# Routing tokens to expert slots in passes of four 128-token tiles that run across batch borders

## The chip, the cores and the metric

The kernel runs on one core of one Trainium2 chip. A core has five engines that work side by side and wait for each other through semaphores: TensorE (PE in the profile; its weight loads are PEld), VectorE (DVE), ScalarE (ACT), GpSimd (POOL) and SyncE (SP, which here only issues DMAs). TensorE writes into PSUM, a small memory of eight banks; the other operands live in SBUF. The metric is the device time of one execution in microseconds (us), lower is better; times of several runs are given by their median.

## The reference

Attention over 8 batches, 8 heads, 576 positions and 64 dimensions, with a window of 128 positions, feeds a soft mixture of experts over all 8 x 576 = 4608 tokens of width 512:

```python
scores = scale * q @ k.T;  scores = where(in_window, scores + bias, -1e9)
attn = exp(scores - max); attn /= sum;  x = (attn @ v) -> [4608, 512]
logits = x @ phi                                   # 32 slots: 8 experts x 4
d = softmax(logits, over tokens);  slot_input = d.T @ x          # [32, 512]
slot_out[e] = relu(slot_input[e] @ w1[e]) @ w2[e]                # 4 rows each
c = softmax(logits, over slots);   return c @ slot_out           # [4608, 512]
```

The softmax over tokens runs over all batches at once, so `slot_input` is built up along the way with a running maximum, a running sum and a rescaled accumulator.

## The kernel before, in words

**Attention.** The work is cut into 72 groups `(b, t, g)`: batch `b`, tile `t` of 128 positions (the fifth, `t = 4`, has the last 64), and half of the heads `g` (the fifth tile takes all heads in one group). That is 9 groups a batch. A loop runs one **round** per group. In round `i` PE does `flip` (L366, transposes of the probabilities of group i-3), `values` (L400, probabilities times v for group i-4) and `scores` (L253 and L260, or L241 and L246) for group i+1; DVE masks (L273 to L277), takes row maxima (L295) and normalises (L311); ACT copies the flipped probabilities out of PSUM (`split`, L373), takes exponentials (`expo`, L351) and copies finished attention outputs (`x_store`, L416); POOL masks the flipped copies (L375, L377) and prepares the sum (L303). SP issues the loads of q, k, v and, spread over the rounds, 36 expert weights of 512 KB.

**Slots.** When a tile of x is complete, `x_flip` (L428) transposes it on PE, and `x_keep` (L437, ACT) copies it out. `flip` and `x_flip` write halves of one PSUM tile, `pq`. When all tiles of a batch are there, a **pass** for this batch begins and takes one step a round: `logits` (L446, four tiles side by side in four strips of 32 rows, the "lanes"), `token_copy` (L464, ACT), `token_max` (L471, DVE), `slot_flip` (L480, PE), `token_exp` (L490 and L494, ACT), `token_sum` (L502, DVE), `token_flip` (L509, PE), `token_keep` (L518, ACT), `slots_max` (L552 and L553, DVE), `slot_sum` (L525, PE), `slots_exp` (L556, ACT), `slot_add` (L538, DVE) and `slots_norm` (L563 and L564 on DVE, L565 on POOL).

**The fifth tile.** The 64-token rests of two batches share one tile, `xt_t`, and belong to the pass of the odd batch (1, 3 and 5; the last batch has another order and its own code behind the loop). That pass has a fifth tile with steps of its own: `logits_tail` (L457), a second copy (L466), second transposes (L482, L511), and `slot_tail` (L532), a matmul that adds to the accumulator of `slot_sum`. Its `x_keep` stands behind `expo` on ACT.

**Order.** The order on each engine is the order in which the code is written: `do(when, i, fn, ...)` files a step under a place of round `i`, and `run(when, i)` writes it there: "pre" is ahead of the round's DVE work, "act" right behind `split`, "mid" and "pe" behind `scores` (ahead of and behind `expo`), "dve" at the end. `after_values` files the steps. After the loop come the last batch and the experts' matmuls.

Of the kernel before, what the change touches and what calls it, by code (L numbers as in the profile page):

```python
# [10 lines left out]
F32 = mybir.dt.float32  # L11
# [5 lines left out]
ALU = mybir.AluOpType  # L17
# [51 lines left out]
def tile_attn_softmoe(  # L69
# [369 lines left out]
    def lanes(b):  # L439
        return 4 if b < last else 2  # L440

    def logits(b):
        lp = ps_1.tile([P, 512], F32, tag="mi", name="lp")
        for j in range(NPAIR):
            for c in range(lanes(b)):
                nc.tensor.matmul(  # L446
                    lp[NS * c:NS * c + NS, 0:P], lhsT=phi[:, j], rhs=xts[c][:, j],
                    start=(j == 0), stop=(j == NPAIR - 1),
                )
        st["l", b] = lp  # L450

    def with_tail(b):
        return b % 2 and b < last

    def logits_tail(b):
        for j in range(NPAIR):
            nc.tensor.matmul(  # L457
                st["l", b][fin, P:2 * P], lhsT=phi[:, j], rhs=xt_t[:, j],
                start=(j == 0), stop=(j == NPAIR - 1),
            )  # L460

    def token_copy(b):
        lp, r = st.pop(("l", b)), NS * lanes(b)
        nc.scalar.copy(lg[0:r, 0:P], lp[0:r, 0:P])  # L464
        if with_tail(b):
            nc.scalar.copy(lg[fin, P:2 * P], lp[fin, P:2 * P])  # L466

    def token_max(b):
        r = NS * lanes(b)
        nm = work.tile([P, 1], F32, tag="nm", name="nm")  # L470
        nc.vector.tensor_reduce(  # L471
            nm[0:r], lgm[0:r, 3:4 + P * (2 if with_tail(b) else 1)], axis=AX.X, op=ALU.max, negate=True)
        st["n", b] = nm

    def slot_flip(b):
        r = NS * lanes(b)
        dp = ps_1.tile([P, 512], F32, tag="mi", name="dp")
        st["d", b] = dp
        lq = dp[:, 2 * P:]
        nc.tensor.transpose(lq[:, 0:r], lg[0:r, 0:P], ident[0:r, 0:r])  # L480
        if with_tail(b):
            nc.tensor.transpose(lq[:, P:P + NS], lg[fin, P:2 * P], ident[fin, fin])  # L482
        st["c", b], st["lm"] = lq, dp

    def token_exp(b):
        r = NS * lanes(b)
        m = P * (2 if with_tail(b) else 1)
        nm = st.pop(("n", b))
        sb = work.tile([P, 1], F32, tag="sb", name="sb")
        nc.scalar.activation(lg[0:r, 0:m], lg[0:r, 0:m], AF.Exp, bias=nm[0:r], scale=1.0, accum_out=sb[0:r])  # L490
        al = None
        if b:
# [13 lines left out]
    def token_flip(b):  # L506
        r = NS * lanes(b)
        dp = st["d", b]
        nc.tensor.transpose(dp[:, 0:r], lg[0:r, 0:P], ident[0:r, 0:r])  # L509
        if with_tail(b):  # L510
            nc.tensor.transpose(dp[:, P:P + NS], lg[fin, P:2 * P], ident[fin, fin])  # L511
# [3 lines left out]
    def token_keep(b):
        dn = work.tile([P, P + NS], F32, tag="dn", name="dn", bufs=1)
        m = P + NS if with_tail(b) else NS * lanes(b)
        (nc.scalar.copy if b < last else nc.vector.tensor_copy)(dn[:, 0:m], st["d", b][:, 0:m])  # L518
        st["d", b] = dn

    def slot_sum(b):
        dn = st["d", b]
        ap = ps_1.tile([P, DM], F32, tag="mi", name="ap") if b < last else pq[:, 0]
        for c in range(lanes(b)):
            nc.tensor.matmul(  # L525
                ap[NS * c:NS * c + NS], lhsT=dn[:, NS * c:NS * c + NS], rhs=xns[c],
                start=True, stop=(c < 3 or not with_tail(b)),
            )
        st["a", b] = ap

    def slot_tail(b):
        nc.tensor.matmul(st["a", b][fin], lhsT=st["d", b][:, P:], rhs=xn_of(b, 4), start=False, stop=True)  # L532

    def slot_add(b):
        ap, r = st.pop(("a", b)), NS * lanes(b)
        al = st.pop(("s", b))[0]
        if b:
# [4 lines left out]
    def rows(b):  # L542
        return slice(9 * (b // 2) + 4 * (b % 2), 9 * (b // 2) + 4 + 5 * (b % 2))

    def slots(b):
        return ln[:, rows(b)]

    def slots_max(b):
        m = 4 + b % 2
        src = st.pop(("c", b))[:, 0:NS * m].rearrange("p (i s) -> p i s", s=NS)  # L550
        cm = work.tile([P, 5], F32, tag="cm", name="cm")
        nc.vector.tensor_reduce(cm[:, 0:m], src, axis=AX.X, op=ALU.max)  # L552
        nc.vector.tensor_tensor(slots(b), src, bc(cm[:, 0:m], 2, NS), op=ALU.subtract)  # L553

    def slots_exp(b):
        nc.scalar.activation(slots(b), slots(b), AF.Exp)  # L556

    def slots_norm(b):
        m = 4 + b % 2
        cs = work.tile([P, 5], F32, tag="cs", name="cs")  # L560
        mul = (nc.gpsimd if b < last else nc.vector).tensor_tensor
        return [
            lambda: nc.vector.tensor_reduce(cs[:, 0:m], lne[:, rows(b)], axis=AX.X, op=ALU.add),  # L563
            lambda: nc.vector.reciprocal(cs[:, 0:m], cs[:, 0:m]),  # L564
            lambda: mul(slots(b), slots(b), bc(cs[:, 0:m], 2, NS), op=ALU.mult),  # L565
# [186 lines left out]
    def after_values(i, key):  # L752
# [9 lines left out]
        tail = with_tail(b)  # L762
        late = b > 0 and b % 2 == 0
        if p == 0 and late:
            do("mid", i + 3, x_flip, b, t)
            do("act", i + 4, x_keep, b, t)
        elif t < 4:
            do("pe", i + 1 + (p == 1 and late), x_flip, b, t)
            if b < last or p == 0:
                do("act", i + 2 + (p == 0 or p == 1 and late), x_keep, b, t)  # L770
        if p == (4 if b < last else 1):
            do("pe", i + 1, logits, b)
            if tail:
# [12 lines left out]
            do("act", i + 5, slots_exp, b)
            if tail:
# [6 lines left out]
            do("dve", i + 6, later, slots_norm, b)  # L794
# [351 lines left out]
```

## Time and profile before

| | |
|---|---|
| median of 3 runs | 301.19 us (300.13, 305.6, 301.19) |
| profiled execution | 298.23 us, span 296.5 us |
| mean granted TensorE clock | 0.979 |
| PE, DVE, ACT, POOL busy | 87%, 74%, 70%, 36% of the span |
| attention rounds | first exponential at 6.49 us, last at about 222 us |
| moved by DMA | 72.62 MB, 245 GB/s over the span |

The span runs from the first to the last instruction. The shares are means over stages with different limits: up to about 222 us four engines work on the rounds, and behind it PE works mostly alone on the experts. A line such as L446 is a line of the kernel before; the profile names a group of instructions by that line, its engine and its tiles.

### The profile page before, as it was taken

The numbers are of one execution on the slowest core, as the hardware profiler recorded it, in microseconds if no ns is written. First come the engines' busy times: TensorE is split into PE (matmuls) and PEld (weight loads), VectorE is DVE, ScalarE is ACT, GpSimd is POOL, SyncE is SP. The second block draws the span as 40 slices with busy tenths as digits, with TensorE's granted clock in tenths as the row PEclk, the third lists the DMA queues.
The fourth block names the chain that finished last, engine by engine and source line by source line (L and its number), as shares of the span: only waits on it lengthen the run. The fifth ranks groups of instructions, "written<-read, shape, count | busy, mean of one in ns | idle before, by whom it ended". The sixth has DMA issues, their size and how long they took to land.

```text
span 296.5 us, 13603 instructions
## 1 busy us (share of the span) xinstructions
PE 257.3 (87%) x5539; PEld 180.4 (61%) x5539; DVE 219.3 (74%) x502; ACT 207.4 (70%) x814; POOL 107.4 (36%) x222
## 2 busy tenths in 40 slices
PE   7587898988889998989889799786988989999980
PEld 3465675766567766757666577465756643587650
DVE  3899997998789999896988998596683444656450
ACT  3789997898789998888997889687684311044450
POOL 2055524543443655254544626365352012000000
PEclk9799999999999999999999999998999999999996
DMA  6736378859675995986797777766455579999996
GB/s 194 223 117 182 92 240 284 248 176 314 204 240 191 303 319 171 312 262 195 207 318 250 229 256 244 234 183 216 132 180 181 165 264 351 411 402 337 342 366 261
DMA packets 36755, 72.62 MB, mean 245 GB/s; under 512 B 4402, under 2 KB 15316, under 8 KB 36692
## 3 DMA queue, kind: packets, MB, share of 16 engines
q1 hardware_dynamic: 35972, 71.24, 72.4%
q8 instruction: 44, 0.72, 1.0%
q10 hardware_dynamic: 720, 0.51, 0.5%
q14 instruction: 19, 0.16, 0.2%
HBM read 62.29 MB, written 9.44 MB: 242 GB/s over the span
## 4 chain that ended last, share of the span: by engine, by line
PE 51%; DVE 19%; ACT 11%; POOL 9%; issue 6%; DMA 2%; DVEq 0%; ACTq 0%; POOLq 0%
PE xp L400 11%; ACT area L351 8%; PE s L260 6%; PE op L990 5%; PE hp L953 5%; DVE s L295 5%; DVE area L311 4%; PE po L1015 3%; PE pq L366 3%; POOL area L375 3%; PE s L253 3%; DVE s L273 3%; POOL area L377 2%; PE lp L446 2%; PE pq L428 2%
## 5 line engine op out<-in xcount | busy, mean ns | idle before, releaser
L351 ACT ACTIVATE area<-s,nb 128x128 f32<-128x128 f32 x286 | 102.4, 384 | 8.8 <-DVE nb L298 8.4
L400 PE MATMUL xp<-area 128*64 128x128 f32 (+1 forms) x1104 | 74.4, 273 | 11.2 <-POOL area L375 3.8
L400 PEld LDWEIGHTS xp<-area 128*64 128x64 f32 x1104 | 54.6, 138 | 20.3 <-POOL area L377 6.3
L351 ACT ACTIVATION_READ_ACCUMULATOR area<-s,nb 128x1 f32 x286 | 63.4, 222 | 0.0
L311 DVE TENSOR_TENSOR area<-area,rs 128x512 f32<-128x512 f32 (+1 forms) x73 | 61.2, 838 | 2.2
L373 ACT COPY area<-pq 128x512 f32<-128x512 f32 (+1 forms) x72 | 42.7, 594 | 18.9 <-PE pq L366 17.0
L295 DVE TENSOR_REDUCE s<-s 128x4 f32<-128x512 f32 x71 | 49.5, 698 | 2.2
L375 POOL TENSOR_SCALAR_AFFINE_SELECT area<-area 128x512 f32<-128x512 f32 x48 | 34.4, 717 | 31.2 <-ACT area L373 30.6
L260 PE MATMUL s<-kq 64*32 64x160 f32 x1792 | 44.0, 303 | 1.3 <-issue 1.1
L303 POOL TENSOR_SCALAR rs<-sm 128x4 f32<-128x4 f32 x70 | 14.0, 200 | 78.7 <-ACT area L351 77.4
L275 DVE COPY_PREDICATED s<-cst,s 128x512 f32<-128x512 int32 x48 | 33.1, 690 | 7.5 <-PE s L260 7.4
L366 PE MATMUL pq<-unit_r,area 64*128 64x64 f32 x552 | 31.1, 231 | 8.3 <-ACT area L437 4.8
L377 POOL TENSOR_SCALAR_AFFINE_SELECT area<-area 128x512 f32<-128x512 f32 x48 | 36.3, 756 | 3.3
L366 PEld LDWEIGHTS pq<-unit_r,area 64*128 64x128 f32 x552 | 23.0, 139 | 23.1 <-ACT area L437 8.3
L260 PEld LDWEIGHTS s<-kq 64*32 64x32 f32 x1792 | 30.1, 107 | 3.3 <-issue 2.7
L416 ACT COPY area<-xp 128x512 f32<-128x512 f32 (+1 forms) x37 | 20.8, 562 | 5.5 <-PE xp L400 5.1
L253 PE MATMUL s<-ramp,ones 64*32 64x320 bf16 x448 | 19.1, 311 | 3.9 <-ACT area L351 2.3
L437 ACT COPY area<-pq 128x512 f32<-128x512 f32 x34 | 20.8, 612 | 0.3 <-PE pq L422 0.3
L1017 ACT COPY ob<-po 128x512 f32<-128x512 f32 x19 | 10.4, 591 | 11.4 <-PE po L1015 11.4
L1017 DVE COPY ob<-po 128x512 f32<-128x512 f32 x17 | 11.2, 687 | 6.6 <-PE po L1015 5.7
L428 PE MATMUL pq<-unit_r,area 64*128 64x64 f32 x264 | 14.8, 232 | 1.1 <-ACT area L437 0.9
L307 DVE RECIPROCAL rs<-rs 128x4 f32<-128x4 f32 (+1 forms) x73 | 12.4, 169 | 4.2 <-POOL rs L303 3.5
(184 smaller groups left out, 329.9 us busy)
## 6 DMA issues: line engine op xcount, KB each, us to landing
w<-w SPq DMA_DIRECT2D x53, 512.0 KB, 5.3
out<-ob SPq DMA_DIRECT2D x36, 256.0 KB, 4.0
kq<-q_t SPq DMA_DIRECT2D x69, 128.0 KB, 3.5
kq<-k_t SPq DMA_DIRECT2D x32, 256.0 KB, 4.1
area<-v_n SPq DMA_DIRECT2D x31, 256.0 KB, 4.7
area<-w SPq DMA_DIRECT2D x8, 512.0 KB, 4.4
area<-v_n SPq DMA_DIRECT2D x12, 128.0 KB, 4.1
kq<-w SPq DMA_DIRECT2D x3, 512.0 KB, 5.4
```

The lines of the kernel that those rows point to most:

```text
L253: nc.tensor.matmul(s4[32 * c:32 * c + 32, 2 * par:2 * par + 2, 32 * r:32 * r + WIN], lhsT=ones[rows, 0:32], rhs=ramp[rows, h], start=True, ...
L260: nc.tensor.matmul(s4[32 * c:32 * c + 32, 2 * par + jj, 32 * r:32 * r + WIN], lhsT=qt[rows, 2 * h + jj if t == 4 else jj, 32 * r:32 * r + 32],
L275: nc.vector.copy_predicated(s4[:, :, P:2 * P], bc(mask_u, 1, 4), s4[:, :, 0:P])
L295: nc.vector.tensor_reduce(st[key]["mx"][:, us], merged(key, us), axis=AX.X, op=ALU.max, negate=True)
L311: nc.vector.tensor_tensor(p4, p4, bc(rs, 2, P), op=ALU.mult)
L351: nc.scalar.activation(s["p4"][:, u], merged(key, u), AF.Exp, bias=s["nb"][:, u:u + 1], scale=SCALE, accum_out=s["sm"][:, u:u + 1],)
L366: nc.tensor.transpose(s["pt"][:, u, r], s["p4"][rows, u], ident[rows, rows])
L373: nc.scalar.copy(pa[:, us].rearrange("p u (r w) -> p u r w", r=2), s["pt"][:, us])
L375: nc.gpsimd.affine_select(pp[:, us], pa[:, us], [[0, m], [-1, P]], ALU.is_gt, 0.0, base=0, channel_multiplier=1)
L377: nc.gpsimd.affine_select(pa[:, us], pa[:, us], [[0, m], [1, P]], ALU.is_ge, 0.0, base=0, channel_multiplier=-1)
L400: nc.tensor.matmul(xp[D * par:D * par + D, j, 0:w], lhsT=v_slot[b, t - 1 + ph][:, D * h:D * h + D], rhs=src[:, 2 * par + i] if t < 4 else ...
L1017: copy_by[by](ob, po)
```

## The change

The seven passes by batch (and the small one of the last batch) become eight passes by readiness (and the small one): the tiles of batches 0 to 6 are put in one list in the order in which they are complete, the shared 64-token tile being an entry like the others, and cut into fours across batch borders; the eighth has three. Every pass has lanes only, so the steps of the fifth tile go. The passes thus begin at other rounds: `logits` at rounds 12, 21, 28, 37, 44, 53, 60 and 66, where it was at 13, 22, 31, 40, 49, 58 and 67. Flips of x are filed at most one a round, at "pe", and each `x_keep` at "act" of the next round; flips for the next pass wait until `slot_sum` of the pass before has been written. `slot_add` is always at "dve" of its round (it was at "pre" for passes without a fifth tile).

```diff
+    tiles = [(b, t) for b in range(last) for t in range(4 + b % 2)] + [(last, 1), (last, 2)]
+    cuts = [4 * k for k in range(8)] + [len(tiles) - 2, len(tiles)]
+    passes = [tiles[a:z] for a, z in zip(cuts, cuts[1:])]
+    end = len(passes) - 1
+    pass_of = {key: (k, c) for k, p in enumerate(passes) for c, key in enumerate(p)}
...
-    def logits(b):
+    def logits(k):
         lp = ps_1.tile([P, 512], F32, tag="mi", name="lp")
         for j in range(NPAIR):
-            for c in range(lanes(b)):
+            for c, key in enumerate(passes[k]):
                 nc.tensor.matmul(
-                    lp[NS * c:NS * c + NS, 0:P], lhsT=phi[:, j], rhs=xts[c][:, j],
+                    lp[NS * c:NS * c + NS, 0:P], lhsT=phi[:, j], rhs=x_of(*key)[:, j],
...
-    def logits_tail(b):
-        for j in range(NPAIR):
-            nc.tensor.matmul(
-                st["l", b][fin, P:2 * P], lhsT=phi[:, j], rhs=xt_t[:, j],
...
-        if with_tail(b):
-            nc.scalar.copy(lg[fin, P:2 * P], lp[fin, P:2 * P])
...
-        if with_tail(b):
-            nc.tensor.transpose(dp[:, P:P + NS], lg[fin, P:2 * P], ident[fin, fin])
-            nc.gpsimd.memset(lg[0:64, P:2 * P], LOW)
-            nc.gpsimd.memset(lg[64:3 * NS, P:2 * P], LOW)
...
-    def slot_tail(b):
-        nc.tensor.matmul(st["a", b][fin], lhsT=st["d", b][:, P:], rhs=xn_of(b, 4), start=False, stop=True)
...
-        tail = with_tail(b)
-        late = b > 0 and b % 2 == 0
-        if p == 0 and late:
-            do("mid", i + 3, x_flip, b, t)
-            do("act", i + 4, x_keep, b, t)
-        elif t < 4:
-            do("pe", i + 1 + (p == 1 and late), x_flip, b, t)
...
-            if tail:
-                do("pe", i + 2, x_flip, b, 4)
-                do("pe", i + 4, x_keep, b, 4)
-                do("pe", i + 5, slot_tail, b)
-                do("dve", i + 5, slot_add, b)
-            else:
-                do("pre", i + 5, slot_add, b)
+        k, c = pass_of[b, t]
+        turn[0] = max(i + 1, turn[0] + 1, ready.get(k - 1, 0) + 4)
+        do("pe", turn[0], x_flip, b, t)
+        if (b, t) != tiles[-1]:
+            do("act", turn[0] + 1, x_keep, b, t)
+        if c == lanes(k) - 1:
+            ready[k] = i
+            do("pe", i + 1, logits, k)
...
+            do("dve", i + 5, slot_add, k)
```

Lines shift by the edit: in the changed kernel `flip` is L372, `values` L406, `scores` L266, `x_flip` L434, `logits` L452, `split` L379, `x_store` L422, `x_keep` L443, `token_copy` L460, `token_exp` L480 and L484, `token_keep` L503, `slots_exp` L536 and `expo` L357.

**PE, end of the round in which the pass over batch 1 begins.** Before, the round ended with `logits` and `logits_tail`, behind the scores of the next group and ahead of the next `flip` and `values`:

```order
L260 MATMUL s_1_84<-kq 32x160 x16
L446 MATMUL lp<-area,phi 32x128 x16
L457 MATMUL lp<-area,phi 32x128 x4
L366 MATMUL pq<-unit_r,area 128x64 x8
L400 MATMUL xp<-area 64x128 x4
```

Now the pass begins one round earlier, on the same round as the last flip of its x:

```order
L266 MATMUL s_0_83<-kq 32x160 x16
L434 MATMUL pq<-unit_r,area 128x64 x8
L452 MATMUL lp<-area,phi 32x128 x16
L372 MATMUL pq<-unit_r,area 128x64 x8
L406 MATMUL xp<-area 64x128 x4
```

The four matmuls of the fifth tile are gone from here; that tile is lane 0 of the next pass.

**ACT, from `token_exp` of the same pass to the second copy of x behind it.** Before:

```order
L490 ACTIVATE lg,sb<-lg,nm 128x256
L494 ACTIVATE al<-lg,nm 128x1
L351 ACTIVATE area,sm<-s_0_83,nb 128x128 x4
L373 COPY area<-pq 128x512
L518 COPY dn<-dp 128x160
L416 COPY area<-xp 128x512
L351 ACTIVATE area,sm<-s_1_84,nb 128x128 x4
L437 COPY area<-pq 128x512
L373 COPY area<-pq 128x512
L556 ACTIVATE ln<-ln 128x4x32
```

Now:

```order
L480 ACTIVATE lg,sb<-lg,nm 128x128
L484 ACTIVATE al<-lg,nm 128x1
L422 COPY area<-xp 128x4x64
L357 ACTIVATE area,sm<-s_0_83,nb 128x128 x4
L379 COPY area<-pq 128x512
L503 COPY dn<-dp 128x128
L357 ACTIVATE area,sm<-s_1_84,nb 128x128 x4
L379 COPY area<-pq 128x512
L536 ACTIVATE ln<-ln 128x4x32
L443 COPY area<-pq 128x512
L422 COPY area<-xp 128x512
```

The copy of the flipped fifth tile out of `pq` stood behind four exponentials (L437 behind L351); it now stands behind `split` and `slots_exp`, ahead of the exponentials.

**PE, near the end of the loop, where the last full pass begins.** Before, ahead of a `values` for batch 7 (the row L400) stood only a flip of x and the flip of the probabilities:

```order
L260 MATMUL s_1_84<-kq 32x160 x16
L428 MATMUL pq<-unit_r,area 128x64 x8
L366 MATMUL pq<-unit_r,area 128x64 x8
L400 MATMUL xp<-area 64x128 x8
L253 LDWEIGHTS ones
```

Now the logits of the last full pass, three lanes, stand ahead of it too; before, they came one round later, behind it:

```order
L266 MATMUL s_1_84<-kq 32x160 x16
L434 MATMUL pq<-unit_r,area 128x64 x8
L452 MATMUL lp<-area,phi 32x128 x12
L372 MATMUL pq<-unit_r,area 128x64 x8
L406 MATMUL xp<-area 64x128 x8
```

**ACT, where the passes take their copy of the logits.** Before, `token_copy` (L464) followed `split` directly, and a copy of x stood elsewhere; now, in the pass that begins at round 28:

```order
L379 COPY area<-pq 128x512
L443 COPY area<-pq 128x512
L460 COPY lg<-lp 128x128
L422 COPY area<-xp 128x512
L357 ACTIVATE area,sm<-s_0_83,nb 128x128 x4
```

One `x_keep` stands ahead of `token_copy` in the same round.

More of the change, by code (lines that the diff above doesn't have):

```diff
@@ L491, in token_exp @@
         al = None
-        if b:
+        if k:
             al = work.tile([P, 1], F32, tag="al", name="al")
@@ L504, in token_sum, with token_flip, token_keep, slot_sum @@
             nc.vector.tensor_copy(s_run, sb)
[L506 to L511, printed above, removed]
-            nc.gpsimd.memset(lg[0:64, P:2 * P], LOW)
-            nc.gpsimd.memset(lg[64:3 * NS, P:2 * P], LOW)
[L515 to L529, printed above, removed]
-    def slot_tail(b):
[L532 to L537, printed above, removed]
+    def token_flip(k):
+        r = NS * lanes(k)
+        nc.tensor.transpose(st["d", k][:, 0:r], lg[0:r, 0:P], ident[0:r, 0:r])
+    def token_keep(k):
+        dn = work.tile([P, P], F32, tag="dn", name="dn", bufs=1)
+        r = NS * lanes(k)
+        (nc.scalar.copy if k < end else nc.vector.tensor_copy)(dn[:, 0:r], st["d", k][:, 0:r])
+        st["d", k] = dn
+    def slot_sum(k):
+        dn = st["d", k]
+        ap = ps_1.tile([P, DM], F32, tag="mi", name="ap") if k < end else pq[:, 0]
+        for c in range(lanes(k)):
+            nc.tensor.matmul(
+                ap[NS * c:NS * c + NS], lhsT=dn[:, NS * c:NS * c + NS], rhs=xns[c], start=True, stop=True)
+        st["a", k] = ap
+    def slot_add(k):
+        ap, r = st.pop(("a", k)), NS * lanes(k)
+        al = st.pop(("s", k))[0]
+        if k:
             nc.vector.scalar_tensor_tensor(acc[0:r], acc[0:r], al[0:r], ap[0:r], op0=ALU.mult, op1=ALU.add)
@@ new lines, in after_values @@
+        if (b, t) not in pass_of:
+            return
+        k, c = pass_of[b, t]
[6 more added lines that the diff above has]
+            do("pe", i + 1, logits, k)
+            if k == end:
+                return
+            assert turn[0] <= i + 3
+            do("act", i + 2, token_copy, k)
+            do("dve", i + 2, token_max, k)
+            do("pe", i + 2, slot_flip, k)
+            do("act", i + 3, token_exp, k)
+            do("dve", i + 3, token_sum, k)
+            do("pe", i + 3, token_flip, k)
+            do("act", i + 4, token_keep, k)
+            do("pre", i + 4, slots_max, k)
+            do("pe", i + 4, slot_sum, k)
+            do("act", i + 5, slots_exp, k)
+            do("dve", i + 5, slot_add, k)
+            do("dve", i + 6, later, slots_norm, k)
@@ L796, in tile_attn_softmoe @@
+    turn, ready = [0], {}
     with tc.manual_schedule(engines=ORDERED):
@@ L837, in tile_attn_softmoe @@
         x_keep(last, 2)
-        token_copy(last)
+        token_copy(end)
         flip(gb, to=bank("pt"))
@@ L841, in tile_attn_softmoe @@
         split(gb, HI)
-        slot_flip(last)
-        token_max(last)
+        slot_flip(end)
+        token_max(end)
         values(ga)
@@ L851, in tile_attn_softmoe @@
         split(gc)
-        token_exp(last)
+        token_exp(end)
         total(gd, LO)
@@ L865, in tile_attn_softmoe @@
         split(gd, HI)
-        token_sum(last)
+        token_sum(end)
         x_store(last, 3)
@@ L869, in tile_attn_softmoe @@
         x_store(last, 4, nc.scalar)
-        token_flip(last)
+        token_flip(end)
         lane_rows(ps_1.tile([P, 512], F32, tag="xp", name="rows"))
@@ L880, in tile_attn_softmoe @@
         x_store(last, 0, js=slice(2, 4))
-        token_keep(last)
+        token_keep(end)
         x_flip(last, 3, free[0])
@@ L887, in tile_attn_softmoe @@
         lane_keep()
-        slot_sum(last)
+        slot_sum(end)
         load_weight()
@@ L897, in tile_attn_softmoe @@
         x_keep(last, 0)
-        slot_add(last)
+        slot_add(end)
         last_flip()
@@ L1040, in tile_attn_softmoe @@
         last_slot_flip()
-        slots_max(last)
-        slots_exp(last)
-        later(slots_norm, last)
+        slots_max(end)
+        slots_exp(end)
+        later(slots_norm, end)
         drain()
```

104 lines of the change are left out of this document (39 added, 65 removed).

## The prediction

> **What bounds the kernel now.** I read the page first: the busy shares, and the chain that ended last.
>
> ```profile
> PE 257.3 (87%) x5539; PEld 180.4 (61%) x5539; DVE 219.3 (74%) x502; ACT 207.4 (70%) x814; POOL 107.4 (36%) x222
> ...
> PE 51%; DVE 19%; ACT 11%; POOL 9%; issue 6%; DMA 2%; DVEq 0%; ACTq 0%; POOLq 0%
> ```
>
> PE carries half of the chain, DVE a fifth. These are averages over the span, so I cut the attention stage at the first exponential of every batch (nine rounds) and, inside a batch, took the five rounds in which `logits` to `slots_exp` stand. The columns are the stretch, its length, busy time of PE, PEld, DVE, ACT and POOL, granted clock, share of the DMA engines and GB/s.
>
> ```profile
> 85.17:110.13 24.96, 23.03 (x596) 17.14 (x592) 23.52 (x53) 23.36 (x97) 12.43 (x26) 1.00 0.81 261
> 110.13:138.48 28.35, 25.72 (x616) 18.74 (x612) 23.26 (x53) 23.64 (x99) 13.55 (x28) 1.00 0.78 249
> ...
> 66.74:85.17 18.43, 16.50 (x346) 11.80 (x338) 13.62 (x31) 14.27 (x58) 8.09 (x18) 1.00 0.79 259
> 120.66:138.48 17.82, 16.45 (x346) 11.90 (x338) 13.48 (x31) 14.16 (x59) 8.10 (x18) 1.00 0.85 271
> 175.75:193.85 18.10, 16.56 (x398) 11.52 (x392) 13.42 (x31) 14.13 (x58) 8.09 (x18) 1.00 0.79 258
> 95.64:110.13 14.49, 13.94 (x326) 10.24 (x318) 13.80 (x31) 13.48 (x57) 7.68 (x16) 1.00 0.94 307
> ```
>
> The last row is a pass without a fifth tile, the three above it are the passes with one. In the last row PE, DVE and ACT are busy for 96%, 95% and 93% of the time: that is what five rounds cost when nothing stands in the way. With the fifth tile they take 18.12 us in the mean, 3.63 us more, and DVE is idle for 4 to 5 us of them though its work is the same. So the passes with a fifth tile are held up by something that is short on DVE and ACT. Outside the rounds nothing of the change is left: behind 241 us the chain is the experts' matmuls, and I take that part as it is.
>
> **The change part by part.** *The fifth tile goes.* The chain over the pass of batch 1 (start, length, what) shows its four PE steps, and the timeline of PE shows a wait of `flip` in each of the three passes.
>
> ```profile
> 66.86 1.08 PE lp L446 x32
> 67.94 0.87 PE lp L457 x8
> ...
> 70.60 0.26 PE dp L480
> 70.86 0.18 PE dp L482
> ...
> 74.56 0.26 PE dp L509
> 74.82 0.19 PE dp L511
> ...
> 81.78 0.99 PE ap L532 x2
> ```
>
> ```profile
> 79.38 0.46 PE L366 MATMUL pq<-unit_r,area 64*128 64x64 f32 x8 [1.18 <-ACT area L437]
> ...
> 132.69 0.46 PE L366 MATMUL pq<-unit_r,area 64*128 64x64 f32 x8 [1.37 <-ACT area L437]
> ...
> 187.78 0.46 PE L366 MATMUL pq<-unit_r,area 64*128 64x64 f32 x8 [1.54 <-ACT area L437]
> ```
>
> One lane alone costs PE nearly what four cost (0.87 against 1.08 us in the logits, 0.99 in `slot_tail`), and the transposes 0.18 and 0.19: 2.23 us a pass. The wait comes from `x_keep` of the fifth tile: it stands behind four exponentials on ACT, and the next `flip` writes the same PSUM tile. At "act" it runs right behind `split` and `slots_exp`, and PE meets it with its scores done as in every other round: 1.36 us in the mean. Together 3.59 us, which agrees with the 3.63 from the windows. Three passes: **-10.8 us**. The floor under that is the last window above: DVE and ACT are then the next to be late, with about 1 us of slack each in five rounds. Bounds: -10.8 if all of it is free, and by the DMA (below) -7.5.
>
> *One more pass comes.* The trace does not show a pass added, but shows what one puts on the chain; this is the pass over batch 4, from its first to its last step.
>
> ```profile
> 149.71 1.01 PE lp L446 x32
> ...
> 156.07 0.26 PE dp L509
> ...
> 159.25 1.04 PE ap L525 x8
> 160.32 0.75 DVE acc L538
> ...
> 166.71 0.19 DVE cs L563
> ...
> 167.67 0.40 POOL ln L565
> ```
>
> That is 3.65 us. Below, it could cost nothing, if PE's parts fall into DVE's turns and the other way round; no gain is possible. Above, the steps of DVE that are not on this chain come on top:
>
> ```profile
> L502 DVE SCALAR_TENSOR_TENSOR fine<-fine,al,sb 128x1 f32<-128x1 f32 x6 | 3.5, 583 | 0.0
> ...
> L553 DVE TENSOR_TENSOR ln<-dp,cm 128x128 f32<-128x128 f32 x4 | 1.2, 292 | 0.1
> L552 DVE TENSOR_REDUCE cm<-dp 128x4 f32<-128x128 f32 x4 | 1.1, 285 | 0.3 <-PE dp L509 0.3
> ```
>
> 0.58, 0.29 and 0.29 make 4.8 us. With engines at 93 to 96% little is hidden, so I take the row of the whole pass: **+3.6 us**.
>
> *The last full pass starts ahead of a DMA wait.* Near the end of the loop `values` of batch 7 waits for v, whose loads are issued at the slot's release, and PE then runs slowly:
>
> ```profile
> 205.68 1.55 PE L400 MATMUL xp<-area 128*64 128x128 f32 x12 [2.35 <-DMA area<-v_n]
> ...
> 208.62 1.17 PE L446 MATMUL lp<-area,phi 128*32 128x128 f32 x32
> ...
> 206.00:207.00 1.00, 1.00 (x12) 0.83 (x8) 0.00 (x0) 0.15 (x2) 0.19 (x1) 0.50 0.16 44
> 207.00:208.00 1.00, 1.00 (x35) 0.65 (x40) 0.00 (x0) 0.00 (x0) 0.00 (x0) 0.50 0.00 0
> 208.00:209.00 1.00, 1.00 (x36) 0.49 (x24) 0.17 (x1) 0.00 (x0) 0.00 (x0) 0.57 0.00 0
> ```
>
> The logits (about 1.1 us) stood behind that wait, on the chain; now they stand ahead of it and fill 1.1 of its 2.35 us: -1.1. The wait itself stays, since the loads are where they were. The granted clock is 0.50, 0.50 and 0.57 in the 3 us behind the wait, so 3 - 1.57 = 1.43 us are lost there. Idle stretches of PE of up to 1.54 us (the row at 187.78) were not followed by a lower clock, and 2.35 - 1.1 = 1.25 is shorter: I take the 1.4 as gained. Together **-2.5 us**, between -1.1 and -2.5.
>
> [...]
>
> *DMA.* The bytes stay and the time shrinks. The clean rounds show a share of 0.94, so their loads have hardly any room. The three passes hold 0.79 x 18.43 = 14.6, 0.85 x 17.82 = 15.1 and 0.79 x 18.10 = 14.3 us of DMA work; at 0.94 that needs 15.5, 16.1 and 15.2 us, together 3.3 us more than three times 14.49. Over a batch the share is only 0.81, and loads can slide into the rounds around: between 0 and +3.3, I take **+1.0 us**.
>
> *Costed at nothing.* The flips of x are as many as before (33), one a round. They are eight transposes like those of `flip`, 0.46 us in the rows above, and a round holds 13.80 / 5 = 2.8 us of DVE beside them; where one meets `slot_sum` (1.04) the two make 1.5 us of PE in a round, which I count within the pass. `slot_add` at "dve" goes behind the round's mask and maximum instead of ahead of them; the next reader of `acc` is a pass later. The six memsets on POOL and the shorter softmax of three passes are off the chain. If the DVE cover is missing, each flip that moved costs its 0.46 us.
>
> **Sum.** -10.8 + 3.6 - 2.5 + 1.0 = -8.7 us against the profiled 298.23 us: 289.5 us. The median of the runs shown is 301.19, 3.0 us above that execution; the same gain there gives **292.5 us**.
>
> **The rivals.** *The clock stays low.* If the half clock behind the v wait has another cause, 1.4 us of the gain go: 293.9. For it: the trace has just this one stretch in the middle of the program, and what starts it is inferred.
>
> *DMA takes the room.* If the loads cannot slide, the three passes end at the 15.5, 16.1 and 15.2 us above: +3.3 instead of +1.0, 294.8, and with the first rival 296.2. For it speaks 0.94; against it, that the clean pass at 0.94 waits for no load.
>
> *Slower: `token_copy` comes late.* In nearly every pass `x_keep` (0.61 us, the second row below) now stands ahead of `token_copy` on ACT; behind it wait `token_max` on DVE, with the next round's mask queued behind, and `slot_flip` on PE, with the next `flip` behind. Where that copy was late before, DVE waited:
>
> ```profile
> 70.36 0.42 DVE L471 TENSOR_REDUCE nm<-lg 128x1 f32<-128x257 f32 x1 [0.77 <-ACT lg L466]
> ...
> L437 ACT COPY area<-pq 128x512 f32<-128x512 f32 x34 | 20.8, 612 | 0.3 <-PE pq L422 0.3
> ```
>
> If all eight passes paid 0.77 us on DVE and the copy's 0.61 on PE, one after the other, 8 x 1.38 = 11.0 us would go, and the time would be 303.5. It decides from 8.7 / 8 = 1.1 us a pass. Against it: that late copy came behind a PE delay, and the clean pass has half a round to spare there.
>
> *More.* Two batches without a fifth tile in their pass lie 1.3 and 1.8 us above the clean one's 24.96:
>
> ```profile
> 29.96:56.23 26.27, 23.87 (x600) 17.57 (x595) 23.52 (x51) 22.82 (x96) 11.95 (x25) 1.00 0.67 209
> ...
> 138.48:165.24 26.76, 23.79 (x596) 17.45 (x592) 23.99 (x53) 23.46 (x98) 12.09 (x26) 1.00 0.77 242
> ```
>
> If the moved `slot_add` and the moved starts also take these 3.1 us away and DMA costs nothing, up to 4 us more: 288.5 to 290.5.
>
> *It does little.* The tails could be hidden by loads altogether: 301. The idle DVE in all three windows speaks against it.
>
> **How the numbers follow.** Forecast 292.5 (290 to 295): 0.38. Clock stays low, 293.9 (292 to 296): 0.20. DMA, 294.8 to 296.2: 0.19. More, 288.5 to 290.5: 0.14. Slower, 303.5: 0.06. Little, 301: 0.03. The range 287.5 to 298 leaves out the last two and the thin ends. A change of 2%, 6 us, is about what a measurement of this kernel can tell from none: faster means below 295.2. Faster: 0.38 + 0.16 + 0.02 + 0.14 = 0.70; slower: 0.03, half of that rival; the same: 0.27.
>
> **What would show it.** In the changed profile no wait of `flip` on `x_keep` over 0.5 us before the last batch; PE's small matmul groups of one lane gone; five rounds from `logits` to `slots_exp` at 14.5 to 16 us everywhere; the matmuls behind the v wait at full clock, and that wait near 1.2 us. I am wrong if new waits for v, q or k appear on PE, if DVE waits on `token_copy` in most passes, or if the batches that hold two passes (from round 53 on) take back more than 4 us.

## The result, and the profile after

The changed kernel takes 291.37 us in the median (291.42, 291.32, 293.68, 291.15) beside 301.62 us of the kernel before in the same comparison: a ratio of 0.969, with a 95% interval of 0.962 to 0.977, or 9.2 us less. The forecast was 292.5 us and a gain of 8.7. Run again beside the experiments below it gave 291.75 (ratio 0.977, 0.971 to 0.982) and 290.49 us (0.969, 0.963 to 0.975). The profiled execution took 291.42 us (its span is 289.4 us), 6.8 us less than the profiled execution before; single executions of either kernel differ by some us, and the last section gives a likely cause.

The busy shares of the changed kernel, and its chain that ended last:

```profile
PE 256.3 (89%) x5535; PEld 179.0 (62%) x5535; DVE 222.4 (77%) x509; ACT 206.2 (71%) x817; POOL 112.3 (39%) x218
...
PE 40%; ACT 18%; DVE 18%; POOL 13%; issue 6%; DMA 2%; DVEq 0%; ACTq 0%; POOLq 0%
```

PE's share of the chain fell from 51% to 40%, that of ACT rose from 11% to 18% and that of POOL from 9% to 13%. In my terms POOL stood only with the 0.40 us of its multiply, inside the pass. The same cut into batches of nine rounds, batches 1 to 6 (counted from 0, as in the code; the expectations below mean batch 2 by "the second batch", and so on), with the columns as before:

```profile
31.05:56.68 25.63, 23.80 (x600) 17.52 (x594) 23.36 (x53) 22.88 (x96) 12.47 (x24) 1.00 0.68 210
56.68:83.18 26.50, 24.09 (x605) 17.49 (x600) 24.51 (x53) 23.34 (x97) 13.85 (x26) 1.00 0.80 252
83.18:111.43 28.25, 24.83 (x592) 17.82 (x588) 23.59 (x53) 23.04 (x97) 14.93 (x28) 0.94 0.75 241
111.43:138.18 26.75, 24.97 (x635) 18.33 (x629) 23.83 (x54) 23.51 (x99) 13.82 (x26) 1.00 0.85 268
138.18:163.36 25.18, 23.43 (x591) 17.32 (x591) 23.67 (x51) 22.87 (x98) 13.38 (x26) 1.00 0.81 252
163.36:191.11 27.75, 25.07 (x660) 17.58 (x660) 24.14 (x57) 23.72 (x102) 13.61 (x27) 1.00 0.80 256
```

Before, these six batches took 26.27, 28.94, 24.96, 28.35, 26.76 and 28.61 us. Batches 2, 4 and 6, which held the fifth tile, are 2.4, 1.6 and 0.9 us shorter, but batch 3, the clean one of 24.96 us, now takes 28.25, at a mean granted clock of 0.94. The five rounds of the first, third, seventh and eighth pass:

```profile
38.89:53.45 14.56, 14.11 (x364) 9.93 (x350) 12.59 (x31) 12.71 (x55) 5.99 (x13) 1.00 0.81 262
...
86.17:102.98 16.81, 16.21 (x426) 11.33 (x422) 13.03 (x31) 13.16 (x56) 5.46 (x13) 0.91 0.68 214
...
180.57:196.63 16.06, 15.85 (x434) 11.36 (x432) 14.05 (x31) 13.85 (x57) 9.12 (x18) 1.00 0.75 242
199.37:214.65 15.28, 13.78 (x274) 10.00 (x272) 13.86 (x31) 12.90 (x55) 9.95 (x18) 1.00 0.58 175
```

Six of the eight lie between 14.5 and 15.4 us, where the passes with a fifth tile had 18.12. Two lie outside the 14.5 to 16 us that the prediction asked for everywhere: the third lost about 1.5 us to the clock (0.91), and in the seventh PE is busy for 15.85 us of the 16.06, which no run explains. At the wait for v the chain, and the clock in the us behind it, read:

```profile
197.69 4.51 DMA area<-v_n
...
202.33 0.88 PE xp L406 x12
...
203.00:204.00 1.00, 1.00 (x45) 0.60 (x41) 0.16 (x1) 0.76 (x5) 0.62 (x2) 1.00 0.08 18
```

The twelve matmuls take 0.88 us where they took 1.55, and the clock stays at 1.00. New, or grown, among the waits of the changed kernel (us in total, times, longest):

```profile
DVE nm L465 <- ACT lg L460: 5.8, 7, 1.4
PE xp L406 <- POOL area L383: 5.8, 18, 0.6
POOL ln L545 <- DVE rs L313: 5.6, 6, 1.5
PE xp L406 <- POOL area L381: 4.7, 6, 1.2
```

The first is the late `token_copy` of my slower rival: six of the eight full passes have it, and the longest of the seven waits, 1.4 us, is that of the small last pass, which has 1.2 us there in the kernel before too. The others belong together: the multiply of `slots_norm` on POOL (L545) waits for DVE, the two masks of the flipped copies (L381, L383) stand behind it in POOL's queue, and `values` (L406) waits for them. The timeline of the changed kernel shows one such place, where batch 3 begins:

```profile
83.05 0.40 POOL L545 TENSOR_TENSOR ln<-ln,cs 128x128 f32<-128x128 f32 x1 [0.91 <-DVE rs L313]
83.13 0.87 DVE L317 TENSOR_TENSOR area<-area,rs 128x512 f32<-128x512 f32 x1
83.41 1.09 POOL L381 TENSOR_SCALAR_AFFINE_SELECT area<-area 128x512 f32<-128x512 f32 x1
84.55 0.44 PE L406 MATMUL xp<-area 128*64 128x128 f32 x4 [1.17 <-POOL area L381]
84.56 0.97 POOL L383 TENSOR_SCALAR_AFFINE_SELECT area<-area 128x512 f32<-128x512 f32 x1
85.59 1.28 PE L406 MATMUL xp<-area 128*64 128x128 f32 x12 [0.60 <-POOL area L383]
```

POOL waits 0.91 us and multiplies for 0.40; PE then waits 1.17 and 0.60 us. The masks are late, and they are slow as well (1.09 and 0.97 us, where the short ones take 0.64); what they overlap with is told under the hardware. The same pair of waits stands where batch 2 begins (from 56.87 us on).

### The profile page after: what moved, and what is told of

The parts are those of the page before. It is cut to its first block, busy times and chain, and to the rows that moved or that the text cites. A ratio compares the mean times of both kernels' runs of the same rounds, so it can differ in the third digit from the quotient of the medians.

```text
span 289.4 us, 13589 instructions
## 1 busy us (share of the span) xinstructions
PE 256.3 (89%) x5535; PEld 179.0 (62%) x5535; DVE 222.4 (77%) x509; ACT 206.2 (71%) x817; POOL 112.3 (39%) x218
## 4 chain that ended last, share of the span: by engine, by line
PE 40%; ACT 18%; DVE 18%; POOL 13%; issue 6%; DMA 2%; DVEq 0%; ACTq 0%; POOLq 0%
ACT area L357 10%; PE xp L406 6%; PE op L963 5%; PE hp L926 5%; DVE area L317 5%; DVE s L301 4%; PE s L266 4%; POOL area L383 4%; POOL area L381 4%; PE po L988 3%; DVE s L281 3%; ACT area L379 3%; ACT area L422 2%; PE lp L452 2%; PE pq L372 2%
## 5 line engine op out<-in xcount | busy, mean ns | idle before, releaser
L357 ACT ACTIVATE area<-s,nb 128x128 f32<-128x128 f32 x286 | 103.1, 394 | 12.3 <-DVE nb L304 10.3
L406 PE MATMUL xp<-area 128*64 128x128 f32 (+1 forms) x1104 | 76.9, 274 | 12.1 <-POOL area L383 5.8
L406 PEld LDWEIGHTS xp<-area 128*64 128x64 f32 x1104 | 54.6, 138 | 23.3 <-POOL area L383 11.0
L357 ACT ACTIVATION_READ_ACCUMULATOR area<-s,nb 128x1 f32 x286 | 66.1, 231 | 0.0
L317 DVE TENSOR_TENSOR area<-area,rs 128x512 f32<-128x512 f32 (+1 forms) x73 | 61.6, 844 | 1.8
L379 ACT COPY area<-pq 128x512 f32<-128x512 f32 (+1 forms) x72 | 43.8, 610 | 14.5 <-PE pq L372 11.9
L266 PE MATMUL s<-kq 64*32 64x160 f32 x1792 | 43.6, 306 | 1.1 <-issue 1.1
L383 POOL TENSOR_SCALAR_AFFINE_SELECT area<-area 128x512 f32<-128x512 f32 x48 | 42.4, 884 | 3.3
L309 POOL TENSOR_SCALAR rs<-sm 128x4 f32<-128x4 f32 x70 | 15.0, 214 | 73.9 <-ACT area L357 72.5
L381 POOL TENSOR_SCALAR_AFFINE_SELECT area<-area 128x512 f32<-128x512 f32 x48 | 34.5, 719 | 16.4 <-ACT area L379 14.8
L372 PE MATMUL pq<-unit_r,area 64*128 64x64 f32 x552 | 31.4, 232 | 3.1 <-ACT area L322 2.6
L266 PEld LDWEIGHTS s<-kq 64*32 64x32 f32 x1792 | 30.1, 108 | 2.6 <-issue 1.9
L372 PEld LDWEIGHTS pq<-unit_r,area 64*128 64x128 f32 x552 | 23.4, 140 | 11.6 <-POOL rs L309 2.9
L422 ACT COPY area<-xp 128x512 f32<-128x512 f32 (+1 forms) x37 | 21.2, 572 | 1.4 <-PE xp L406 0.8
L443 ACT COPY area<-pq 128x512 f32<-128x512 f32 x34 | 20.8, 612 | 0.3 <-PE pq L428 0.3
L434 PEld LDWEIGHTS pq<-unit_r,area 64*128 64x128 f32 x264 | 11.1, 140 | 13.0 <-issue 9.2
```

The costliest lines, as they stand in the source:

```text
L266: nc.tensor.matmul(s4[32 * c:32 * c + 32, 2 * par + jj, 32 * r:32 * r + WIN], lhsT=qt[rows, 2 * h + jj if t == 4 else jj, 32 * r:32 * r + 32],
L317: nc.vector.tensor_tensor(p4, p4, bc(rs, 2, P), op=ALU.mult)
L357: nc.scalar.activation(s["p4"][:, u], merged(key, u), AF.Exp, bias=s["nb"][:, u:u + 1], scale=SCALE, accum_out=s["sm"][:, u:u + 1],)
L372: nc.tensor.transpose(s["pt"][:, u, r], s["p4"][rows, u], ident[rows, rows])
L379: nc.scalar.copy(pa[:, us].rearrange("p u (r w) -> p u r w", r=2), s["pt"][:, us])
L381: nc.gpsimd.affine_select(pp[:, us], pa[:, us], [[0, m], [-1, P]], ALU.is_gt, 0.0, base=0, channel_multiplier=1)
```

## The experiments

Three were made on the kernel before (e1, e2 and e9), the others on the changed one. Ratios are to runs of the kernel before on the same chip, medians in us; where one stretch settles a term, I read it from stretches at full clock.

**e1: the copy of the fifth tile earlier (kernel before).**

```diff
-                do("pe", i + 4, x_keep, b, 4)
+                do("act", i + 5, x_keep, b, 4)
```

> The kernel before, with one step moved: the copy of the flipped fifth tile out of pq (x_keep) runs right behind split, one round later by its file number, ahead of the exponentials instead of behind them. By my sum the three waits of flip on it (1.18, 1.37 and 1.54 us) go and nothing else changes: 4.1 us faster than before, so about 297 us beside a before of 301. If loads have no room (the DMA theory), the waits turn into waits of values or scores for v, q or k, and the gain stays under 1.5 us. If the copy of x now holds back the exponentials of its round instead, the gain is about 3 x 0.6 us smaller, 2.3 us.

Measured: 297.39 beside 300.24, ratio 0.989 (0.985 to 0.993), 3.3 us less. The five rounds of the three passes with a fifth tile:

```profile
65.26:81.84 16.58, 16.41 (x346) 11.77 (x338) 13.85 (x31) 14.01 (x58) 8.38 (x18) 1.00 0.85 282
117.26:133.84 16.58, 16.58 (x346) 11.92 (x338) 13.91 (x31) 14.04 (x58) 8.39 (x18) 1.00 0.89 291
172.89:189.46 16.57, 16.54 (x398) 11.52 (x392) 13.85 (x31) 14.01 (x58) 8.38 (x18) 1.00 0.85 283
```

16.58 three times, 1.54 us under the mean of 18.12. The three waits of `flip` on `x_keep` are gone; what the list still has there, 0.7 us over three places, the kernel before has as well. PE is now busy throughout, and 16.58 - 14.49 = 2.09 us are left. So the split of the term into a wait and PE work is shown, but the 2.09 are not only the four PE steps, for which I counted 2.23: these windows also hold one flip of x more than the clean one (24 matmuls of L428 against 16, 0.45 us of PE), and that flip stays in the changed kernel. The agreement of 3.59 with 3.63 in the prediction has the same flip in it and is partly chance. Of the 4.6 us in these windows not all reach the end: in this profile a wait of `values` in batch 5 is 2.40 us where it was 1.03, and the wait for v 2.77 us where it was 2.35, both followed by half clock.

**e2: no fifth tile at all (kernel before).** `with_tail` returns False, so the steps of the fifth tile are left out. With them go its flip and its copy of x (240 matmuls of L428 instead of 264), which the changed kernel keeps.

> The kernel before with the steps of the fifth tile left out of its three passes and not put anywhere else; 192 tokens do not reach the slots, so the output differs. By my sum this is worth 3 x 3.59 = 10.8 us: about 290.5 us beside a before of 301. If the loads have no room, 3.3 us of it are lost: 7.5 us, 293.5. If the gain is over 12 us, the cost of the fifth tile was more than its PE steps and its flip wait.

Measured: 288.93, ratio 0.967 (0.961 to 0.972): 10.0 us less, 8.3 to 11.7. The interval holds 10.8 and not 7.5; but three flips of 0.46 us, 1.4 us in all, may be in the 10.0 that the change does not save. The first of the three passes, at full clock:

```profile
65.88:80.59 14.71, 14.15 (x318) 10.09 (x312) 13.97 (x31) 13.03 (x56) 7.64 (x16) 1.00 0.91 299
```

14.71 us with the DMA engines at 0.91: the loads did find their room. The other two (17.45 and 17.14 us) each hold a pause of PE of 1.85 and 1.50 us without a releaser and a stretch of half clock, at mean clocks of 0.90.

**e3: one pass less (changed kernel).** The steps of the fourth pass are left out, those of all others stay.

> The changed kernel with every step of one full pass left out (the fourth, whose logits stand at round 37; its flips and copies of x stay); its 512 tokens do not reach the slots, so the output differs. By my sum a pass costs 3.65 us: about 287.7 us beside 291.4 of the changed kernel. If a pass hides in the turns of the other engines, 0 to 1 us. If the steps of DVE beside the chain count in full, 4.8 us: 286.6.

Measured: 290.53, ratio 0.964 (0.957 to 0.970); the changed kernel in the same comparison has 291.75 and 0.977. The medians give 1.2 us for a pass and the ratios 3.9, which decides nothing. Batch 4, in which that pass stands, does (the changed kernel run again, then this one):

```profile
112.37:139.08 26.71, 24.94 (x635) 18.30 (x629) 23.81 (x54) 23.45 (x99) 13.79 (x26) 1.00 0.85 271
```

```profile
113.04:137.53 24.49, 22.91 (x593) 17.19 (x589) 23.26 (x47) 22.25 (x94) 13.69 (x23) 1.00 0.89 290
```

2.2 us, not 3.65: PE loses 2.0 us of work, the rest of the pass lay beside other work.

**e4: the changed kernel again.**

> The changed kernel unaltered, to stand beside the others on the same chip: 291.4 us, and the same stretch of half clock in its third batch (3.41 us from about 86 us) if that comes from what the kernel does; if it is chance, it is absent or elsewhere and the time is 1.7 us lower.

Measured: 291.75. The half clock stands elsewhere, in batch 2 and not in batch 3. What that means is told under the hardware.

**e5: the last full pass a round later.**

```diff
         if c == lanes(k) - 1:
+            i += k == end - 1
             ready[k] = i
             do("pe", i + 1, logits, k)
...
-            do("dve", i + 5, slot_add, k)
+            do("pre" if k == end - 1 else "dve", i + 5, slot_add, k)
```

> The changed kernel with only its last full pass one round later (and its slot_add at pre, as before the change), so that its logits stand again behind the wait for v. By my sum that gives back the term of the hole: the wait of values for v is near 2 us again instead of 0.96, a stretch of half clock follows it, and the time is 2.5 us higher than the changed kernel's 291.5, 294. If the half clock has another cause than the wait, the wait is longer but the clock stays full: 1.1 us higher, 292.6. If the wait only moves because v comes later or earlier by itself, no difference beyond 0.5 us.

Measured: 292.57, ratio 0.975 (0.969 to 0.981), which by itself is not told from the changed kernel. The rounds from the start of the last batch to the last but one, in the changed kernel and here, and behind them the window with the wait, the one after it, and the wait on PE:

```profile
191.11:214.65 23.54, 22.04 (x510) 16.30 (x504) 22.00 (x49) 20.68 (x87) 13.61 (x25) 1.00 0.61 186
```

```profile
189.79:215.66 25.87, 23.12 (x508) 16.83 (x500) 21.86 (x49) 20.75 (x87) 13.87 (x26) 0.93 0.55 172
...
197.05:200.47 3.42, 1.80 (x60) 1.17 (x52) 3.16 (x9) 2.94 (x12) 2.38 (x6) 1.00 0.91 294
200.47:203.88 3.41, 3.03 (x55) 2.04 (x58) 1.07 (x3) 1.56 (x9) 1.75 (x3) 0.50 0.20 61
```

```profile
199.42 0.44 PE L406 MATMUL xp<-area 128*64 128x128 f32 x4 [1.00 <-POOL area L381]
200.85 1.54 PE L406 MATMUL xp<-area 128*64 128x128 f32 x12 [0.99 <-DMA area<-v_n]
```

2.3 us more (the changed kernel's other two profiles have 23.78 and 24.32 there, so 1.6 to 2.3), and the half clock is back. The wait for v is not near 2 us, as expected, but 0.99, as in the changed kernel; what came back is a wait of 1.00 us on POOL's mask just ahead of it, which the logits (1.07 us) cover in the changed kernel. Idle time up to the landing of v is 1.99 us against 0.96: the pass's place fills the hole, as the sum had it. What the sum had too simply is the clock: neither stretch is longer than the 1.54 us that it took for harmless, and half clock followed.

**e6: `token_copy` ahead of `x_keep`.**

```diff
-            do("act", i + 2, token_copy, k)
+            todo.setdefault(("act", i + 2), []).insert(0, (token_copy, (k,)))
```

> The changed kernel with token_copy ahead of x_keep on ACT in the round behind the logits. The waits of DVE's maximum on token_copy (5.8 us in seven places in the changed profile, 2.2 in three before) should shrink to about 2. If they are on the path that sets the end (the rival of the late copy), the time falls by up to 3.6 us, to 288. By my sum they are covered by the slack of the other engines: 0 to 1 us, 290.5 to 291.5; the copy of x is then late instead, and the next flip may wait for it.

Measured: 291.22, ratio 0.972 (0.967 to 0.977). The wait, and batches 2 to 4:

```profile
DVE nm L465 <- ACT lg L460: 2.7, 6, 1.4
```

```profile
57.19:83.69 26.50, 23.92 (x606) 17.52 (x600) 24.68 (x53) 23.34 (x97) 13.85 (x26) 1.00 0.82 268
83.69:110.46 26.77, 23.34 (x592) 17.00 (x588) 23.59 (x53) 23.04 (x96) 14.93 (x28) 1.00 0.74 238
110.46:137.22 26.76, 25.00 (x635) 18.43 (x629) 23.81 (x54) 23.52 (x99) 13.83 (x26) 1.00 0.82 268
```

3.1 us of DVE's wait are gone (1.4 of the 2.7 left are those of the small last pass), and the batches are as long as without the edit to 0.03 us (26.50 and 26.75 us for batches 2 and 4 in the first profile, 26.74 for batch 3 in e4). In these batches the late copy costs nothing: the rival is refuted, and 3.1 us of a wait in the list were worth zero.

**e7: the multiply of `slots_norm` on DVE.**

```diff
-        mul = (nc.gpsimd if k < end else nc.vector).tensor_tensor
+        mul = nc.vector.tensor_tensor
```

> The changed kernel with the multiply of slots_norm on DVE instead of POOL. In the changed profile it stands on POOL ahead of the two masks of the flipped copies, and values waits for those 1.17 and 0.60 us in the second and again in the third batch. If that multiply is the cause, both waits shrink to what other rounds show (0.3 to 0.6 us in all), the half clock behind them goes, and batches 2 and 3 are 1.2 us shorter each, 2.9 with a stretch of half clock: 2 to 4 us in all, 287.5 to 289.5. If DVE then is the bound, 8 multiplies of about 0.3 us come back: 290 to 293.

Measured: 288.35, ratio 0.959 (0.953 to 0.965), the fastest of all: 2.9 to 4.2 us under e5, e6 and e8 of the same comparison, and 2.1 to 3.4 under the changed kernel in the other ones. Of the waits on the two masks, those on L381 are gone from PE's list, and those on L383 fell from 5.8 us to 4.4. That row, and batches 3 and 4:

```profile
PE xp L406 <- POOL area L383: 4.4, 13, 0.6
```

```profile
83.19:108.23 25.04, 22.59 (x584) 16.70 (x582) 23.52 (x54) 23.16 (x96) 12.40 (x24) 1.00 0.80 254
108.23:133.78 25.55, 24.58 (x630) 18.31 (x627) 24.17 (x54) 23.59 (x99) 12.79 (x25) 1.00 0.83 264
```

The two batches take 26.77 and 26.76 us in e6, so 1.7 and 1.2 us more; batch 2 is only 0.5 us shorter (25.95 against 26.50), though the same pair of waits stood there. Why it gains less is open.

**e8: `slots_norm` two rounds later**, still on POOL.

> The changed kernel with all three parts of slots_norm two rounds later, the multiply still on POOL. If the place (a round in which POOL masks late) is what matters and not the engine, the waits of 1.17 and 0.60 us go here too: 2 to 4 us faster, 287.5 to 289.5. If any round has the same masks, the waits move two rounds on and the time stays at 291.5.

Measured: 291.91, ratio 0.973 (0.967 to 0.979): no gain. The waits left the rounds at 57 and 83 us, and came back in another:

```profile
108.80 0.40 POOL L545 TENSOR_TENSOR ln<-ln,cs 128x128 f32<-128x128 f32 x1 [0.91 <-DVE rs L313]
109.15 1.09 POOL L381 TENSOR_SCALAR_AFFINE_SELECT area<-area 128x512 f32<-128x512 f32 x1
110.29 0.44 PE L406 MATMUL xp<-area 128*64 128x128 f32 x4 [1.17 <-POOL area L381]
```

Batch 3 shrank to 25.22 us, nearly as far as in e7, with the multiply still on POOL; there it now waits 0.37 us for DVE (at 88.51). Batch 4 grew to 28.71, of which up to 1.7 are a stretch of half clock. So neither the engine nor the round does it alone: the multiply costs PE where it stands ahead of the masks and waits long for DVE, 0.91 us at each of the three pairs. Batch 2, whose pair went too, did not shrink (26.76 us against 26.50).

**e9: the same multiply on DVE, in the kernel before.** The edit is that of e7.

> The kernel before with the multiply of slots_norm on DVE instead of POOL, as in the changed kernel where it brought 3 to 5 us. In the kernel before, that multiply waits 0.5 to 0.6 us for DVE in six rounds, and values waits 0.6 us behind it, 3.75 us in all. If the loss is one that the change brought (its passes put the multiply into rounds where POOL waits 0.9 to 1.5 us), the kernel before gains little: 0 to 1.5 us, 298.5 to 300. If it was there before, the kernel before gains as much as the changed one: 3 to 5 us, 295 to 297.

Measured: medians of 300.9 (12 runs) and 300.94 (17 runs). The interval of the ratio (1.008 to 1.024) rests on two runs of the kernel before, one of them its fastest by 3.6 us, so I go by the medians: no gain. (The means are no further apart than 0.3 us; by the scatter of the runs, an estimate, a gain of 1 us could hide, one of 3 could not.) In the profile batches 2 and 3 are not shorter either, 30.36 and 26.26 us against 28.94 and 24.96, of which 1.69 and 0.73 are pauses of PE of the kind told in the last section. What e7 took back is in the main a cost that the change had brought.

**e10 and e11: `slots_norm` behind the loop, and one pass less with it.**

> The changed kernel with slots_norm of all passes in one piece on DVE behind the loop, ahead of the experts' first transposed copies, where DVE is idle for more than half of the time. In the loop 7 x (0.28 + 0.16) us go from DVE, 7 x 0.40 from POOL with its waits for DVE. If DVE sets the rounds where PE does not wait, it is 1 to 3 us below the kernel with the multiply on DVE (288.35 beside a before of 299.4): 285.5 to 287.5. If only the mask behind the multiply mattered, the same as that one. If the one large norm (about 3 us) lands on the experts' path, 290 to 291.

> The kernel with slots_norm behind the loop, and every step of the fourth full pass left out (its flips and copies of x stay; its 512 tokens do not reach the slots, so the output differs). What a pass costs, without the norm: 2.2 us by the fourth batch of the run with one pass less (26.73 to 24.48 us), 3.1 us by my sum (3.65 less the 0.19 + 0.40 of the norm).

Measured: e10 292.59, ratio 0.971 (0.964 to 0.979), a miss; e11 291.23, 0.970 (0.964 to 0.976). In the built order the norm of 31 tiles came to stand in the loop's last round instead of behind it, and ran in pieces between the steps of that round's maximum, as the timeline of e11 shows:

```profile
207.24 1.20 DVE L544 TENSOR_REDUCE cs<-ln 128x31 f32<-128x1023 f32 x1
...
209.85 1.44 DVE L546 TENSOR_TENSOR ln<-ln,cs 128x992 f32<-128x992 f32 x1
211.45 0.37 ACT L357 ACTIVATE area<-s,nb 128x128 f32<-128x128 f32 x1 [3.01 <-DVE nb L304]
213.49 0.90 PE L367 MATMUL pq<-unit_r,area 128*128 128x128 f32 x3 [3.54 <-ACT area L443]
```

The last exponentials wait 3.01 us, PE 3.54 (1.03 in the changed kernel), and two stretches of half clock follow. What the loop would gain without the norm is thus not to be read from the time. Batch 4 still tells what a pass costs without its norm, in e10 and then in e11:

```profile
110.84:136.42 25.58, 24.64 (x633) 18.31 (x627) 23.71 (x51) 23.49 (x98) 13.19 (x25) 1.00 0.87 283
```

```profile
107.85:132.28 24.43, 22.72 (x591) 17.17 (x585) 23.28 (x47) 22.27 (x92) 13.12 (x23) 1.00 0.86 280
```

1.15 us. With e3: 2.2 us a pass, of which about 1.1 come with its norm, and e7, where only the multiply left POOL, puts 1.2 us of the same batch down to that.

**e12: the changed kernel again.**

> The changed kernel unaltered, beside the others: 291.5 us. Its waits of values for the masks behind the multiply (1.17 and 0.60 us in the second and in the third batch) are there again, and a stretch of half clock follows in none, one or both of these batches, as the fixed 3.41 us windows happen to lie.

Measured: 290.49; the four waits are there (1.17 and 0.60 us, twice), and no half clock behind either pair.

## Why the prediction was right, point by point

The time (292.5 forecast, 290.5 to 291.8 measured) and the sign were right, and so was the mechanism of the largest term. That the sum hit so closely is partly luck: the pass (by 1.4 us) and the DMA (by 1.0) were charged too much, the fifth tile was credited with 0.8 us or more too much, and the 2.2 us of POOL's multiply in batches 2 and 3 were missed.

- *The fifth tile, -10.8:* right in kind, somewhat too large. e2 gives -10.0 (8.3 to 11.7), e1 1.54 us of wait (1.36 forecast) and 2.09 us of PE work (2.23) a pass. Both hold the flip of the fifth tile, which the change keeps; without it the term is between -8.6 and -10.0, an estimate from e2 less three flips of 0.46 us. Among the waits of PE's matmuls in the changed kernel, `flip` (L372) no longer waits for `x_keep`.
- *One more pass, +3.6:* too much. e3 gives 2.2. The step that failed was "with engines at 93 to 96% little is hidden": a chain through PE, DVE, ACT and POOL is not added to the rounds in full. Between e10 and e11 PE loses 1.9 us of work in batch 4, and the batch only 1.15 us. Its lower bound of 0 and upper one of 4.8 held.
- *The last full pass ahead of the wait for v, -2.5:* right within its bounds; e5 gives -1.6 to -2.3, and the wait, forecast near 1.2 us, is 0.96. The reason given for the clock was not right: it compared single idle stretches (1.54 us harmless, 2.35 not), and e5 fell to half clock behind two of 1.00 and 0.99 us.
- *DMA, +1.0:* nothing of it is seen. No wait for q or k is among PE's waits, that for v shrank, and e2's first pass ran at a share of 0.91 in 14.71 us. The rival that DMA takes the room is refuted with it.
- *Clock stays low:* refuted where I put it, by e5. But half clock came elsewhere, which no case of mine held.
- *Slower by `token_copy`:* the wait came, in six of the eight full passes, and e6 shows the price of 3.1 us of it, zero. The prediction had named this wait as a sign that it is wrong; the sign came, and the forecast held, so the sign was a bad one.
- *More:* batch 1 fell from 26.27 to 25.63 us and batch 5 from 26.76 to 25.18, 2.2 of the 3.1 us that this rival spoke of. No run tried `slot_add` or the starts by themselves, so the cause stays open.
- *What I missed:* "costed at nothing" did not ask where `slots_norm` falls. Its multiply moved with the passes into rounds in which POOL waits longer for DVE. In the kernel before it waited 0.47 to 0.59 us in each of six rounds (the first one below); in the changed one it waits 0.91 us where batches 2 and 3 begin, and up to 1.50 later:

```profile
58.66 0.40 POOL L565 TENSOR_TENSOR ln<-ln,cs 128x128 f32<-128x128 f32 x1 [0.59 <-DVE rs L307]
```

By e7 this costs 0.5, 1.7 and 1.2 us in batches 2, 3 and 4, the last of them already within the 2.2 of a pass.

Summed from the runs: -10.0 + 2.2 - 2.0 + 0.5 + 1.7 = -7.6 us, taking 2.0 as the middle of e5's, or -6.2 with the -8.6 for the fifth tile. The three ratios give -9.2, -7.0 and -9.2, so up to 3.0 us are not accounted for; the two batches under *More* could be 2.2 of them.

## What to carry to other kernels

Before moving a chain of steps, list every instruction of it on every engine, the small ones on an idle engine too, and look at what stands behind each in that engine's queue at the new place: here 0.4 us of work on an engine that was busy for 39% of the time held up the busiest engine by 1.8 us in one round. A wait in the list is worth only what lies on the path: 3.1 us on DVE were worth nothing, and the same 1.8 us on PE were worth 1.7 in one batch and 0.5 in another. The cheapest way to tell is to take one step away and compare the length of the same batch, not the whole time. The best kernel of this study is the changed one with that multiply on DVE (288.35 us).

## What the runs showed of the hardware

**The granted clock changed on a grid of 3.413 us, and idle pieces in one window add up.** Between two changes of the granted clock lie 3.413, 191.146, 3.413 and 81.920 us in the profile before (1, 56, 1 and 24 times 3.413), and 6.827, 68.267, 3.413 and 194.560 us in the one after (2, 20, 1 and 57 times). The kernel doesn't set where the grid lies: from the first instruction, a window of half clock begins at 85.91 us in the first profile of the changed kernel and at 60.06 in e4, 25.85 us apart, which is 7.57 windows. The pair of idle stretches of 1.17 and 0.60 us stands in all three profiles of the changed kernel, and in these half clock followed where both fell into one window. The window with the pair and the one behind it, in the first profile (batch 3), in e4 (batch 2) and in e12 (batch 3):

```profile
82.50:85.91 3.41, 1.64 (x28) 1.26 (x28) 3.26 (x8) 2.62 (x11) 2.64 (x5) 1.00 0.84 241
85.91:89.33 3.42, 3.42 (x71) 2.26 (x70) 1.93 (x5) 1.51 (x8) 1.77 (x3) 0.50 0.43 157
```

```profile
56.65:60.06 3.41, 1.65 (x30) 1.10 (x26) 3.33 (x8) 2.81 (x11) 2.41 (x3) 1.00 0.81 257
60.06:63.47 3.41, 3.41 (x61) 2.39 (x62) 1.62 (x5) 1.50 (x8) 1.99 (x4) 0.50 0.42 135
```

```profile
81.30:84.70 3.40, 2.14 (x34) 1.67 (x34) 3.35 (x8) 3.36 (x14) 2.18 (x5) 1.00 0.92 284
84.70:88.10 3.40, 2.80 (x90) 2.22 (x92) 2.88 (x7) 1.76 (x9) 2.62 (x5) 1.00 0.52 178
```

With PE busy for 1.64 or 1.65 us of the window the next one runs at 0.50; with 2.14 it stays at 1.00, as with 2.16 where batch 3 of e4 begins (83.95 to 87.37 us). No one figure of idle time divides the windows: half clock followed 2.12 us of it (before, from 202.04), 1.77 and 1.76 (above), 1.62 (e5, above) and, behind the loop of the changed kernel, 1.46 (from 280.47); full clock followed 1.59 and 1.54 (before, from 219.10 and 184.97). (A window that was at half clock already, from 10.82 us in the changed kernel, was followed by another with only 0.56 us idle.) Each window at half clock costs up to 1.7 us, an estimate from half of its 3.41; batch 3 took 28.25 us with one, and 26.74 and 26.73 without (e4, e12). The 17 runs of the kernel before beside e9 to e12 show mean granted clocks of 0.959 to 0.986; over 300 us that is 8 us of full clock, nearly five such windows, and by this estimate up to 8 us of scatter between executions of one kernel (their times are 294.27 to 305.77 us).

**PE pauses that nothing releases.** The "issue" gaps of over 0.7 us inside a group of matmuls are three between 10 and 225 us in the profiles before and after: 0.96 and 0.75 us before (at 48.87 and 72.95), and 1.08 us in the changed kernel (at 174.56). They end 1.55, 1.29 and 1.41 us after a transfer of the instruction queue q8 landed, though that queue has only 44 and 43 transfers in these executions. That PE waits there for its instructions is my guess, and no run tested it.

**A mask on POOL and a normalise on DVE took longer when they overlapped.** By itself a mask of 128x512 takes 0.64 us and a normalise (L317) 0.69, the medians of the 53 masks and 38 normalises beside which the other doesn't run, in the profiles before and after. In these two 90 masks started while a normalise ran, and 68 of them took over 0.8 us; of the 102 others 3 did. All 68 ended 0.49 to 0.51 us behind the end of that normalise, though they had started from 0.08 to 0.66 us into it; and a normalise that started while a mask ran took 0.96 us in the median and up to 1.15. The first mask of the timeline above is such a case: the multiply delayed it into the normalise. The kernel before has 26 masks over 0.8 us, the changed one 45, which is likely part of why the waits on L383 grew. What makes the two slow each other is not shown: no run here took the DVE work away to test it.
